# A joint run for the h of two groups, V0 in quads by other queues, and a later place for the loads of batch 2

## The chip, the cores and the metric

The kernel runs on one core of one Trainium2 chip. Five engines work side by side and meet at semaphores: TensorE (PE, matmuls; its weight loads are listed as PEld), VectorE (DVE), ScalarE (ACT), GpSimd (POOL) and SyncE (SP, which here only issues transfers). The metric is the device time of one execution in microseconds (us); less is better.

## The reference

```python
x = softmax-weighted causal convolution of x_in over 7 taps   # weights per head: 8 heads of 24 channels
xt = x.transpose(0, 2, 1)
h = xt @ U @ V                       # U: seq x 32, V: 32 x seq, along the sequence
u = x + h.transpose(0, 2, 1)
out = u + np.maximum(u @ w_ch1, 0.0) @ w_ch2     # 192 -> 768 -> 192
```

There are 8 batches of 4224 positions with 192 channels, all float32 at the kernel's edge.

## The kernel before

**Tiling.** A batch is 33 tiles of 128 positions. The 264 tiles of all batches form 33 groups of eight, so groups 0 to 3 lie wholly in batch 0. In the text below, y is the convolved x, tt is U^T y (32 x 192, kept four times on 128 partitions), h is V's part of tt, u = y + h, uT is u transposed (channels on partitions), and rl is the output of the first channel matmul after the relu.

**Stages.** The convolution is done by PE with banded weight matrices made at the start (line 369 for batches 0 and 1, line 339 with 32-row bands for the others, from a second, shifted copy `xb_sb` of x that POOL makes in lines 293 to 305). `tt_mm` (402), `tt_split`, `tt_sum` and `tt_done` make tt. `h_tiles` (457, 479) makes u for a group; `transp` (498) has SP issue a transposing transfer that makes uT. `w1` (554) multiplies uT by W1, and ACT and DVE evict it with the relu (568, 570); `w2` (583, 592, 600) multiplies by W2, adds u on DVE and has SP issue the output. All PSUM tiles come from one ring of eight banks (`bank`), in order of allocation.

**Groups 0 and 1** are made in another way, with no transposing transfer. `yT_part` (509) lets PE transpose y of a group into PSUM banks, through matmuls with an identity, half the tiles to partitions 0 to 63 and half to 64 to 127. `hT_part` (524) adds V0^T tt to the same banks with 32-row matmuls that all take tt and V0 from partitions 0 to 31, and evicts the sums to uT (256, 258). `parts` is a list of (channel block c, first tile, end tile, bank, evicting engine). Group 0 has five parts, group 1 three; the order on PE, with lines of the listing, is

```python
yT_part(0, parts0)      # 729
conv_piece(1); tt_mm; tt_split; conv_piece(2); ...
yT_part(0, more[0:1]); tt_late(ps0); yT_part(0, more[1:])
yT_part(1, parts1); tt_done(0, ps0)
hT_part(0, parts0 + more)
yT_part(1, rest); hT_part(1, parts1 + rest)
```

**What sets the order.** The schedule is written out by hand, each engine works through its instructions in program order. All loads of x, U, V and the weights are issued by POOL, in one queue, and convert float32 to bfloat16 on the way: x of batch 0 in three pieces with U between, then V0 (line 133), W1, the first part of batch 1, V, W2, the rest of batch 1. SP issues the small conv weight `w_sb` (61) first, and later the transposes and the outputs. A batch of x is four parts (`XP`), held in two buffers.

`SLOTS` says for each slot which groups go through `w1`, which through `w2`, and what stands between the pieces of `w2` (four pieces of two tiles for each group): h0 is u of group 0, d1 the convolution of batch 1, c2 that of batch 2, t and s make tt, x2:6 are six copies of POOL for batch 2, l2:3 is the load of part 3 of batch 2, held until the last `w2` piece issued so far is done. `LOADS` names loads that are held until a given (group, m) of `w1` is done. The loads of batch 2 stand in both: parts 0 and 1 behind the last m of `w1` of group 1, part 2 behind the first `w2` piece of group 0, part 3 behind its second.

Of the kernel before, what the change touches and what calls it, by code (L numbers as in the profile page):

```python
# [8 lines left out]
ACT = mybir.ActivationFunctionType  # L9
BF16 = mybir.dt.bfloat16  # L10
F32 = mybir.dt.float32
# [3 lines left out]
def kernel(  # L15
# [20 lines left out]
    GT = 8  # L36
# [3 lines left out]
    HB = P // 2  # L40
# [4 lines left out]
    cst = ctx.enter_context(tc.tile_pool(name="cst", bufs=1))  # L45
# [4 lines left out]
    uts = ctx.enter_context(tc.tile_pool(name="uts", bufs=5))  # L50
# [5 lines left out]
    def bank():  # L56
        return psp.tile([P, 512], F32, name="ps", tag="ps")


    w_sb = cst.tile([P, H, KC], F32, name="w_sb")  # L60
    nc.sync.dma_start(out=w_sb[:], in_=weight[:].partition_broadcast(P))
    xt = [None] * B
    yt = [None] * B

# [38 lines left out]
    def iota(t, pattern, base, mul):  # L103
# [20 lines left out]
        out=Ur[:, 0:nfull, :], in_=U4[0 : nfull * P, :].rearrange("(k p) c -> p k c", p=P)  # L124
# [4 lines left out]
        x_piece(k)  # L129


    V0_sb = cst.tile([R, 2 * GT * P], BF16, name="V0_sb")
    nc.gpsimd.dma_start(out=V0_sb[:], in_=moe_V[:, 0 : 2 * GT * P])
    W1_sb = cst.tile([P, 3, M4], BF16, name="W1_sb")
    for m0, m1 in ((0, 2 * P), (2 * P, M4)):
        for hf in range(2):
            nc.gpsimd.dma_start(
                out=W1_sb[HB * hf : HB * hf + HB, :, m0:m1],
                in_=moe_w_ch1[:, m0:m1].rearrange("(c k) m -> k c m", k=HB),
# [27 lines left out]
    for hh in range(2):  # L167
# [3 lines left out]
        out=dif[:], in0=dif[:], scalar1=rq[:, 0:1], scalar2=None, op0=ALU.add  # L171
# [5 lines left out]
        out=d_sb[:],  # L177
# [3 lines left out]
    )  # L181
    e_sb = cst.tile([P, H, KC], F32, name="e_sb")
    nc.scalar.activation(e_sb[:], d_sb[:], ACT.Exp)
    hot = cst.tile([P, KC, BW], BF16, name="hot")
    nc.vector.tensor_tensor(
        out=hot[:],
# [6 lines left out]
        out=ident[:], in0=fp[:], scalar1=float(P), scalar2=None, op0=ALU.is_equal  # L193
# [9 lines left out]
        out=c_sb[:].rearrange("p k h -> p h k"),  # L203
# [5 lines left out]
    for hh in range(2):  # L209
# [3 lines left out]
            out=pr[:],  # L213
# [8 lines left out]
        out=Eq[:], in0=efp[:], scalar1=rq[:, 1:2], scalar2=None, op0=ALU.is_equal  # L222
# [3 lines left out]
        out=fp[:], in0=fp[:], scalar1=R - 1, scalar2=None, op0=ALU.bitwise_and  # L226
# [3 lines left out]
        out=R4[:], in0=fp[:], scalar1=0.0, scalar2=None, op0=ALU.is_equal  # L230
# [23 lines left out]
    def evac(eng, out, in_):  # L254
        if eng == "A":
            nc.scalar.activation(out=out, in_=in_, func=ACT.Copy)  # L256
        else:
            nc.vector.tensor_copy(out=out, in_=in_)  # L258
# [135 lines left out]
    ttb = [[] for _ in range(B)]  # L394
# [25 lines left out]
    def tt_done(b, p):  # L420
        t = sml.tile([P, D], BF16, name="tt_sb", bufs=3)
        nc.vector.tensor_copy(out=t[:], in_=p[:, 0:D])
        ttb[b] = t
# [14 lines left out]
    uTt = [None] * NG  # L438
# [64 lines left out]
    def yT_part(g, parts):  # L503


        for c, i0, i1, p, _ in parts:
            for i in range(i0, i1):
                for hf in range(2):
                    nc.tensor.matmul(  # L509
                        out=p[HB * hf : HB * hf + HB, (i - i0) * P : (i - i0 + 1) * P],  # L510
                        lhsT=yt[0][:, GT * g + 4 * hf + i, HB * c : HB * c + HB],
                        rhs=ident[:],
                        start=(i == i0),
                        stop=False,
                        tile_position=(0, HB * hf),
                    )

    def hT_part(g, parts):

        uTt[g] = uts.tile([P, 4, 3, P], BF16, name="uT")  # L520
        for c, i0, i1, p, _ in parts:
            for hf in range(2):
                t0 = (2 * g + hf) * 4 * P
                nc.tensor.matmul(  # L524
                    out=p[HB * hf : HB * hf + HB, 0 : (i1 - i0) * P],
                    lhsT=ttb[0][0:R, HB * c : HB * c + HB],
                    rhs=V0_sb[:, t0 + i0 * P : t0 + i1 * P],
                    start=False,
                    stop=True,
                    tile_position=(0, HB * hf),  # L530
                )
        for c, i0, i1, p, eng in parts:
            evac(
                eng,
                uTt[g][:, i0:i1, c, :],
                p[:, 0 : (i1 - i0) * P].rearrange("p (i t) -> p i t", t=P),
            )

    RELU = ["AD", "AD", "AA", "AD", "AD", "AD"]
    RELU0 = ["AA", "AD", "AA", "AD", "AA", "AD"]  # L540
# [1 line left out]
    def w1(g, pat):  # L542
        rl = rls.tile([P, MC, 2, 4 * P], BF16, name="rl_sb")
        rlt[g] = rl
        ends = []
        lead = 2 if g == 0 else 1
        order = [(m, c) for c in range(3) for m in range(lead)]
        order += [(m, c) for m in range(lead, MC) for c in range(3)]
        pps = {}
        for m, c in order:  # L550
            if c == 0:
                pps[m] = [bank(), bank()]
            for hf in range(2):
                last = nc.tensor.matmul(  # L554
                    out=pps[m][hf][:],
                    lhsT=W1_sb[HB * hf : HB * hf + HB, c, m * P : (m + 1) * P],
                    rhs=uTt[g][HB * hf : HB * hf + HB, :, c, :],
                    start=(c == 0),
                    stop=(c == 2),
                    tile_position=(HB * hf, 0),  # L560
                )
            if c < 2:
                continue
            pp = pps[m]
            ends.append(last)
            for hf in range(2):
                if pat[m][hf] == "A":
                    nc.scalar.activation(out=rl[:, m, hf, :], in_=pp[hf][:], func=ACT.Relu)  # L568
                else:
                    nc.vector.tensor_scalar_max(out=rl[:, m, hf, :], in0=pp[hf][:], scalar1=0.0)  # L570
        return ends
# [38 lines left out]
    def x_load(b, q, after):  # L610
# [7 lines left out]

    SLOTS = [
        ([0], [], {}),  # L620
        ([1], [0], {0: ["h0"], 1: ["h3", "l2:2"], 2: ["l2:3"]}),
        ([2], [1], {0: ["d1", "h1"], 1: ["t1"], 3: ["s1"], 4: ["h4", "x2:6"]}),
        ([3], [2], {1: ["h5"], 3: ["h6"]}),
        (
            [4, 5],
# [41 lines left out]
        SLOTS.append((gs, gs, {p: [w for w in what if w] for p, what in at.items()}))  # L667
    assert nh == NG

    LOADS = {2: [(1, 5), (1, 5)], 3: [(4, 1), (4, 4), (5, 1), (5, 4)]}  # L670
    for b in range(4, B):
        g = 3 * b - 6
        LOADS[b] = [(g, 0), (g, 3), (g + 1, 0), (g + 1, 3)]

# [4 lines left out]
    def tt_late(p):  # L679

        for n, j in enumerate(late):
            nc.tensor.matmul(
                out=p[:, 0:D],
                lhsT=U4_sb[:, n, :, :].rearrange("p a r -> p (a r)"),
                rhs=yt[0][:, j, :],
                start=False,
                stop=(n + 1 == len(late)),
            )
# [10 lines left out]
    for r, (k0, k1) in KP[2].items():  # L699
        j = NB0 // 2 * r + k0  # L700
        nc.gpsimd.tensor_copy(
            out=U4_sb[:, o : o + k1 - k0, :, :],
            in_=U_sb[:]
# [9 lines left out]
    for q in range(4):  # L713
        src = moe_V[:, 0 : full * 8 * P].rearrange("r (k q t) -> r k q t", q=4, t=2 * P)
        nc.gpsimd.dma_start(
            out=V_sb[32 * q : 32 * q + 32, 0 : 2 * full, :].rearrange(
                "r (k a) t -> r k (a t)", a=2
            ),
            in_=src[:, :, q, :],
# [3 lines left out]
        out=V_sb[0:32, 2 * (NT // 8), :], in_=moe_V[:, (NT - 1) * P : NT * P]  # L723
# [1 line left out]
    W2_sb = cst.tile([P, MC, D], BF16, name="W2_sb")  # L725
    nc.gpsimd.dma_start(out=W2_sb[:], in_=moe_w_ch2[:].rearrange("(m p) d -> p m d", p=P))

    parts0 = [(0, 0, 2, bank(), "A"), (0, 2, 4, bank(), "D"), (1, 0, 4, bank(), "D")]
    yT_part(0, parts0)
    def conv_piece(k):  # L730
        for n, h in enumerate(range(0, H, 3)):
            for r in KP[k]:
                conv(0, h, min(3, H - h), [r], "AD"[n % 2], KP[k], {r: work[n]})
# [5 lines left out]
    ps0 = work[3]  # L739
    for n, part in enumerate(ttb[0]):  # L740
        nc.tensor.matmul(out=ps0[:, 0:D], lhsT=R4[:], rhs=part[:], start=(n == 0), stop=False)
    more = [(2, 0, 2, bank(), "A"), (2, 2, 4, bank(), "A")]
    yT_part(0, more[0:1])
    tt_late(ps0)
    yT_part(0, more[1:])
    parts1 = [(0, 0, 4, bank(), "A")]
    yT_part(1, parts1)
    tt_done(0, ps0)
    hT_part(0, parts0 + more)
    rest = [(c, 0, 4, bank(), "ADA"[c]) for c in (1, 2)]  # L750
    yT_part(1, rest)
    hT_part(1, parts1 + rest)
    band2 = cst.tile([P, H, QB], BF16, name="band2")
    for xp in XP[1:]:
        x_part(1, *xp)
    for r in range(4):
        q = slice(QB * r, QB * r + QB)
        for hh in range(2):
            nc.gpsimd.tensor_copy(
                out=band2[q, HQ * hh : HQ * hh + HQ, :],  # L760
                in_=bands[hh][q, :, HB * (r % 2) : HB * (r % 2) + QB],
# [86 lines left out]
```

## Time and profile before

| | |
|---|---|
| median of 3 runs | 325.0 us (324.93 to 325.19) |
| profiled execution, first to last instruction | 323.2 us |
| PE busy (share of the span) | 317.6 us (98%) |
| DVE / ACT / POOL busy | 268.6 / 170.0 / 142.7 us |
| granted clock of PE, mean | 1.000 |
| x of batch 0, first piece | issued from 1.27 us on, first conv matmul that needed it 9.63 us |
| L509 (y transposed), 48 matmuls | 0.22 us each |
| L524 (h of groups 0 and 1), 16 matmuls | 0.33 us each, 18.34 to 20.5 us |
| uT evictions of groups 0 and 1 | ACT 5, DVE 3 |
| loads of batch 2 issued | 29.29, 30.1, 30.95 and 32.66 us |

The profile is one execution, and its span leaves out what lies before the first and after the last instruction. Busy shares are over the whole span. A matmul's length contains the time it takes to leave the array, so matmuls that follow each other overlap in the profile, and the distance of their starts tells the pace. A transfer is told by its issue (on SP, ACT or POOL) and by the time to its landing.

### The profile page before, as it was taken

Reading aid. Unit: us, or ns where it says so; the run is one execution under the profiler, and the core shown is the slowest. Engines: PE = TensorE matmul, PEld = TensorE weight load, DVE = VectorE, ACT = ScalarE, POOL = GpSimd, SP = SyncE. Lnnn points to the kernel's source line nnn. Section 1 sums busy time; section 2 is a strip of 40 time slices with the busy share of each in tenths; the row PEclk is TensorE's granted clock in tenths of the full one; section 3 lists DMA queues with packets and bytes.
Section 4 is the critical chain, followed back from the end, with each engine's and each line's share of the span. In section 5 each row is a group of like instructions: output and inputs, shape, how many; then the busy total and the mean of one; then the engine's idle time right before and its main releaser. Section 6 shows DMA issues by size and latency. Waiting matters only on the chain.

```text
span 323.2 us, 9583 instructions
## 1 busy us (share of the span) xinstructions
PE 317.6 (98%) x3996; PEld 223.7 (69%) x3996; DVE 268.6 (83%) x551; ACT 170.0 (53%) x344; POOL 142.7 (44%) x111
## 2 busy tenths in 40 slices
PE   8999999999999999999999999999999999999995
PEld 3747676478677647866864884687797497487495
DVE  6769989987977986997898699789888897896863
ACT  1766724860874397088239609824903902912910
POOL 8764179728957983992897497000000000000000
PEclk9999999999999999999999999999999999999999
DMA  9999993999998999599499957138268059048035
GB/s 106 192 191 183 206 209 100 196 192 257 208 135 200 246 142 190 166 189 209 130 237 192 181 149 194 52 105 231 61 178 262 3 150 275 18 121 271 2 121 173
DMA packets 122906, 53.51 MB, mean 166 GB/s; under 512 B 87760, under 2 KB 122832, under 8 KB 122864
## 3 DMA queue, kind: packets, MB, share of 16 engines
q1 hardware_dynamic: 84528, 38.08, 45.4%
q0 software_dynamic: 38192, 14.73, 39.2%
q8 instruction: 31, 0.51, 0.7%
q10 hardware_dynamic: 144, 0.10, 0.1%
q14 instruction: 11, 0.09, 0.1%
HBM read 29.49 MB, written 25.95 MB: 172 GB/s over the span
## 4 chain that ended last, share of the span: by engine, by line
PE 92%; ACT 3%; DMA 2%; DVE 1%; issue 0%; POOL 0%; POOLq 0%
PE ps L583 42%; PE ps L554 39%; PE ps L339 3%; PE ps L457 3%; DMA x_sb<-in_x_dram 2%; PE ps L402 2%; ACT rl_sb L568 2%; PE ps L369 1%; ACT y_sb L256 1%; PE ps L509 1%; DVE u_sb L479 1%; DVE rl_sb L570 1%; PE ps L524 0%; PE ps L428 0%; POOL x_sb L79 0%
## 5 line engine op out<-in xcount | busy, mean ns | idle before, releaser
L568 ACT ACTIVATE rl_sb<-ps 128x512 bf16<-128x512 f32 x233 | 124.3, 604 | 108.0 <-PE ps L554 96.0
L583 PE MATMUL ps<-W_sb,rl_sb 128*128 128x192 bf16 x1584 | 141.2, 246 | 0.2
L583 PEld LDWEIGHTS <-rl_sb 128*128 128x128 bf16 x1584 | 128.3, 98 | 11.8 <-issue 11.5
L554 PE MATMUL ps<-uT,W_sb 64*128 64x512 bf16 x1188 | 131.7, 376 | 0.0
L570 DVE TENSOR_SCALAR rl_sb<-ps 128x512 bf16<-128x512 f32 x163 | 105.3, 688 | 15.7 <-PE ps L554 15.4
L554 PEld LDWEIGHTS <-W_sb 64*128 64x128 bf16 x1188 | 66.9, 94 | 60.4 <-issue 3.9
L592 DVE TENSOR_TENSOR out_sb<-ps,u_sb 128x384 f32<-128x384 f32 (+1 forms) x133 | 70.4, 551 | 25.5 <-PE ps L583 25.0
L305 POOL COPY xb_sb<-x_sb 32x3072 bf16<-32x3072 bf16 (+1 forms) x24 | 67.4, 2824 | 0.5
L479 DVE TENSOR_TENSOR u_sb<-y_sb,ps 128x192 bf16<-128x192 bf16 (+1 forms) x168 | 66.3, 461 | 0.0
L293 POOL COPY xb_sb<-x_sb 128x3072 bf16<-128x3072 bf16 x12 | 32.7, 2742 | 42.1 <-PE ps L339 32.2
L256 ACT ACTIVATE y_sb<-ps 128x384 bf16<-128x384 f32 (+4 forms) x90 | 38.3, 520 | 9.7 <-PE ps L339 7.4
L79 POOL DMA_DIRECT2D x_sb<-in_x_dram x32 | 27.0, 848 | 9.6 <-PE ps L457 3.8
L258 DVE CAST y_sb<-ps 128x408 bf16<-128x408 f32 (+4 forms) x36 | 19.1, 578 | 1.3 <-PE ps L369 1.0
L457 PE MATMUL ps<-tt_sb,V_sb 32*128 32x192 bf16 x264 | 12.4, 246 | 0.1
L339 PE MATMUL ps<-x_sb,band 64*32 64x384 bf16 x192 | 12.1, 333 | 0.0
L339 PE MATMUL ps<-xb_sb,band 64*32 64x384 bf16 x192 | 12.1, 332 | 0.0
L457 PEld LDWEIGHTS <-V_sb 32*128 32x128 bf16 x264 | 4.7, 92 | 7.3 <-issue 7.3
L416 ACT ACTIVATE tt_hi<-ps 128x192 bf16<-128x192 f32 x8 | 2.6, 330 | 11.9 <-PE ps L402 11.9
L369 PE MATMUL ps<-x_sb,band 64*64 64x240 bf16 (+3 forms) x192 | 8.0, 276 | 0.2 <-DMA x_sb<-in_x_dram 0.2
L339 PEld LDWEIGHTS <-band 64*32 64x32 bf16 x384 | 4.5, 89 | 5.2 <-issue 2.4
L153 PE MATMUL ps<-zz 128*128 128x512 f32 (+1 forms) x10 | 6.7, 816 | 1.1 <-DVE zz L143 1.1
L369 PEld LDWEIGHTS <-band 64*64 64x64 bf16 x192 | 6.0, 106 | 2.1 <-issue 1.4
(65 smaller groups left out, 71.3 us busy)
## 6 DMA issues: line engine op xcount, KB each, us to landing
out_dram<-out_sb SPq DMA_DIRECT2D x131, 192.0 KB, 2.7
x_sb<-in_x_dram POOLq DMA_DIRECT2D x14, 384.0 KB, 6.9
x_sb<-in_x_dram POOLq DMA_DIRECT2D x7, 432.0 KB, 6.7
x_sb<-in_x_dram POOLq DMA_DIRECT2D x7, 408.0 KB, 8.0
x_sb<-in_x_dram POOLq DMA_DIRECT2D x1, 504.0 KB, 7.3
uT<-u_sb SPq DMA_TRANSPOSE x31, 3.5
x_sb<-in_x_dram POOLq DMA_DIRECT2D x1, 480.0 KB, 5.6
W_sb<-in_moe_w_ch_dram POOLq DMA_DIRECT2D x2, 192.0 KB, 7.8
```

The lines of the kernel that those rows point to most:

```text
L79: return nc.gpsimd.dma_start(out=xt[b][HB * r : HB * r + HB, s0:s1, :], in_=x[b, blk * HB : (blk + s1 - s0) * HB, :].rearrange("(j p) d -> ...
L256: nc.scalar.activation(out=out, in_=in_, func=ACT.Copy)
L293: nc.gpsimd.tensor_copy(out=xbt[b][:, s0:s1, :], in_=xt[b][:, s0 + 1 : s1 + 1, :])
L305: nc.gpsimd.tensor_copy(out=xbt[b][q, s0:s1, :], in_=xt[b][q, s0:s1, :])
L339: nc.tensor.matmul(out=pp[r][QB * cg : QB * cg + QB, 0 : nk[r] * GS], lhsT=w[hr], rhs=t[hr, st : st + 2 * nk[r] - 1 : 2, hs], start=True, ...
L457: nc.tensor.matmul(out=banks[pr][:, a * D : (a + 1) * D], lhsT=V_sb[32 * q : 32 * q + 32, (j // 8) * 2 + j % 2, :], rhs=ttb[b][32 * q : 32 ...
L479: nc.vector.tensor_tensor(out=u_group(g)[:, i : i + n, :, hf, :], in0=yt[b][:, run[0] : run[0] + n, :].rearrange("p n (c k) -> p n c k", c=3),
L554: last = nc.tensor.matmul(out=pps[m][hf][:], lhsT=W1_sb[HB * hf : HB * hf + HB, c, m * P : (m + 1) * P], rhs=uTt[g][HB * hf : HB * hf + HB ...
L568: nc.scalar.activation(out=rl[:, m, hf, :], in_=pp[hf][:], func=ACT.Relu)
L570: nc.vector.tensor_scalar_max(out=rl[:, m, hf, :], in0=pp[hf][:], scalar1=0.0)
L583: last = nc.tensor.matmul(out=cps[:, a * D : (a + 1) * D], lhsT=rlt[g][:, m, hf, (i + a) * P : (i + a + 1) * P], rhs=W2_sb[:, m, :], start ...
L592: nc.vector.tensor_tensor(out=o[:, 0:n, :].rearrange("p n (c k) -> p n c k", c=3), in0=cps[:, 0 : n * D].rearrange("p (n c k) -> p n c k", ...
```

## The change

1. V0 is no longer loaded by POOL. Four transfers of 32 rows by 512 columns, issued at the start by SP (two) and ACT (two), bring it as float32 onto four blocks of 32 partitions, ahead of the first issue of x in the program. ACT casts it to bfloat16 in one instruction behind the exponential of the conv weights.
2. Groups 0 and 1 have three parts each, of one whole bank. `yT_part` of group 1 stands wholly ahead of the h matmuls. `hT_part` takes both groups at once: for each channel block four matmuls of 512 columns, one on each block of 32 rows (q), the halves of group 0 on q = 0 and 1, those of group 1 on q = 2 and 3. The evictions follow, group 0 first, each group by ACT, DVE, ACT.
3. The loads of batch 2 leave `LOADS`. Part 0 stands behind the third `w2` piece of group 0, parts 1 and 2 behind the fourth, part 3 behind the first `w2` piece of group 1.

```diff
     nc.sync.dma_start(out=w_sb[:], in_=weight[:].partition_broadcast(P))
+    V0_f = cst.tile([4 * R, 4 * P], F32, name="V0_f")
+    for q in range(4):
+        (nc.scalar if q % 2 else nc.sync).dma_start(
+            out=V0_f[R * q : R * q + R, :], in_=moe_V[:, 4 * P * q : 4 * P * (q + 1)]
+        )
...
-    V0_sb = cst.tile([R, 2 * GT * P], BF16, name="V0_sb")
-    nc.gpsimd.dma_start(out=V0_sb[:], in_=moe_V[:, 0 : 2 * GT * P])
...
     nc.scalar.activation(e_sb[:], d_sb[:], ACT.Exp)
+    V0_sb = cst.tile([4 * R, 4 * P], BF16, name="V0_sb")
+    nc.scalar.activation(out=V0_sb[:], in_=V0_f[:], func=ACT.Copy)
...
-    def hT_part(g, parts):
...
+    def hT_part(of):
+        for c in range(3):
+            for g in range(2):
+                p = of[g][c][1]
+                for hf in range(2):
+                    q = 2 * g + hf
+                    nc.tensor.matmul(
+                        out=p[HB * hf : HB * hf + HB, :],
+                        lhsT=ttb[0][R * q : R * q + R, HB * c : HB * c + HB],
+                        rhs=V0_sb[R * q : R * q + R, :],
+                        start=False,
+                        stop=True,
+                        tile_position=(R * q, HB * hf),
+                    )
+        for g in range(2):
+            uTt[g] = uts.tile([P, 4, 3, P], BF16, name="uT")
+            for c, p, eng in of[g]:
+                evac(eng, uTt[g][:, :, c, :], p[:].rearrange("p (i t) -> p i t", t=P))
...
-        ([1], [0], {0: ["h0"], 1: ["h3", "l2:2"], 2: ["l2:3"]}),
-        ([2], [1], {0: ["d1", "h1"], 1: ["t1"], 3: ["s1"], 4: ["h4", "x2:6"]}),
+        ([1], [0], {0: ["h0"], 1: ["h3"], 3: ["l2:0"], 4: ["l2:1", "l2:2"]}),
+        ([2], [1], {0: ["d1", "h1"], 1: ["t1", "l2:3"], 3: ["s1"], 4: ["h4", "x2:6"]}),
...
-    LOADS = {2: [(1, 5), (1, 5)], 3: [(4, 1), (4, 4), (5, 1), (5, 4)]}
+    LOADS = {3: [(4, 1), (4, 4), (5, 1), (5, 4)]}
...
-    parts0 = [(0, 0, 2, bank(), "A"), (0, 2, 4, bank(), "D"), (1, 0, 4, bank(), "D")]
-    yT_part(0, parts0)
+    parts0 = [(c, bank(), "ADA"[c]) for c in range(3)]
+    yT_part(0, parts0[0:2])
...
-    more = [(2, 0, 2, bank(), "A"), (2, 2, 4, bank(), "A")]
-    yT_part(0, more[0:1])
+    yT_part(0, parts0[2:])
     tt_late(ps0)
-    yT_part(0, more[1:])
-    parts1 = [(0, 0, 4, bank(), "A")]
+    parts1 = [(c, bank(), "ADA"[c]) for c in range(3)]
     yT_part(1, parts1)
     tt_done(0, ps0)
-    hT_part(0, parts0 + more)
-    rest = [(c, 0, 4, bank(), "ADA"[c]) for c in (1, 2)]
-    yT_part(1, rest)
-    hT_part(1, parts1 + rest)
+    hT_part([parts0, parts1])
```

More of the change, by code (lines that the diff above doesn't have):

```diff
@@ L503, in yT_part @@
     def yT_part(g, parts):
-        for c, i0, i1, p, _ in parts:
-            for i in range(i0, i1):
+        for c, p, _ in parts:
+            for i in range(4):
                 for hf in range(2):
                     nc.tensor.matmul(
-                        out=p[HB * hf : HB * hf + HB, (i - i0) * P : (i - i0 + 1) * P],
+                        out=p[HB * hf : HB * hf + HB, i * P : (i + 1) * P],
                         lhsT=yt[0][:, GT * g + 4 * hf + i, HB * c : HB * c + HB],
                         rhs=ident[:],
-                        start=(i == i0),
+                        start=(i == 0),
                         stop=False,
@@ L516, in yT_part @@
                     )
-    def hT_part(g, parts):
[L520 to L530, printed above, removed]
-                )
[L532 to L537, printed above, removed]
+    def hT_part(of):
[15 more added lines that the diff above has]
+            for c, p, eng in of[g]:
+                evac(
+                    eng,
+                    uTt[g][:, :, c, :],
+                    p[:].rearrange("p (i t) -> p i t", t=P),
+                )
     RELU = ["AD", "AD", "AA", "AD", "AD", "AD"]
```

## The prediction

> **What bounds the kernel now.** Read first: the page's busy times. TensorE (PE) is busy 317.6 of 323.2 us and its clock row is full throughout, so time can only come off where PE starts late or waits. Second: the chain of waits in order of time. From 81 us on it is PE alone, in a fixed period of 28 us per batch; whatever is won or lost before then reaches the end undiminished unless a transfer stands in between. The start of the chain:
>
> ```profile
> 2.29 7.30 DMA x_sb<-in_x_dram
> ...
> 17.47 0.18 issue
> 17.65 0.24 PE ps L682
> 17.89 0.46 PE ps L509 x12
> 18.35 0.83 PE ps L524 x10
> 19.18 0.57 PE ps L509 x16
> 19.75 0.76 PE ps L524 x6
> 20.51 1.23 PE ps L554 x10
> 21.74 3.04 ACT rl_sb L568 x6
> 24.79 0.04 issue
> 24.83 4.16 PE ps L554 x36
> ```
>
> The reader sees start and length of each piece: x must land (9.6 us), then PE runs to the h stage (L509 transposes y, L524 adds h: 18.35 to 20.51), then `w1` of group 0 fills its first banks, and for 3.04 us ScalarE (ACT), not PE, sets the pace, until its sixth rl eviction frees the bank with which `w1` of group 1 starts (24.83). Third, the timeline there and at the start (start, length, engine, line; idle time before in brackets):
>
> ```profile
> 10.60 0.45 PEld L369 LDWEIGHTS <-band 64*64 64x64 bf16 x20 [0.21 <-DVE band L258]
> 17.82 0.53 PE L509 MATMUL ps<-ident,y_sb 128*64 128x128 bf16 x12
> 19.68 0.83 PE L524 MATMUL ps<-V_sb,tt_sb 32*64 32x512 bf16 x6
> 20.12 1.08 ACT L256 ACTIVATE uT<-ps 128x512 bf16<-128x512 f32 x2 [0.35 <-PE ps L524]
> 21.73 3.54 ACT L568 ACTIVATE rl_sb<-ps 128x512 bf16<-128x512 f32 x7 [0.52 <-PE ps L554]
> 24.44 0.34 PE L457 MATMUL ps<-tt_sb,V_sb 32*128 32x192 bf16 x8
> ```
>
> ACT was idle 0.52 us before its rl run: it waited for PE. If uT is ready earlier, ACT's run begins earlier, and all after it moves by that. Fourth, the windows of the start (DMA share and GB/s last), and the timeline of the transfers of the middle:
>
> ```profile
> 2.50:3.00 0.50, 0.50 (x2) 0.06 (x1) 0.00 (x0) 0.00 (x0) 0.50 (x1) 1.00 0.09 20
> 3.00:3.50 0.50, 0.50 (x2) 0.27 (x1) 0.00 (x0) 0.00 (x0) 0.41 (x3) 1.00 0.86 52
> 4.50:5.00 0.50, 0.50 (x2) 0.33 (x1) 0.50 (x3) 0.25 (x1) 0.50 (x1) 1.00 1.59 191
> ```
>
> ```profile
> 41.04 1.45 SPq L498 DMA_TRANSPOSE uT<-u_sb  x1
> 45.35 2.74 POOL L293 COPY xb_sb<-x_sb 128x3072 bf16<-128x3072 bf16 x1 [1.41 <-DMA x_sb<-in_x_dram]
> 48.69 11.24 POOL L305 COPY xb_sb<-x_sb 32x3072 bf16<-32x3072 bf16 x4
> ```
>
> The DMA engines are nearly empty until 3.0 us (share 0.09, full is 1.6). The transpose for group 3, issued at 41.04, lands 5.6 us later, at 46.64, and `w1` of group 3 begins at 47.12: 0.48 us of slack. POOL's copies of batch 2 end at 59.93 and are first read at 66.88.
>
> **V0 by the hardware queues.** Two more issues on SP after w_sb's, two on ACT ahead of the table load, about 0.40 us each (w_sb's L61; ACT's own last issue took 0.38). ACT's table load ends at 2.8 instead of 2.03; its first work, e_sb, starts at 4.71 after 2.68 us idle, which hides it. SP has nothing else until 27.14. POOL loses one issue of 0.56 us, and V0's bytes leave the queue ahead of W1; W1's last part lands at 18.9 already, before `w1` (20.45), so this gains nothing. The new cast of 128x512 on ACT costs 0.60 (its uT evictions); it waits for V0, then stands before the band evictions at 8.03, with ACT idle from 4.96: hidden if V0 lands by 7.4, otherwise it delays the bands. The four transfers are 256 KB together. What they take from x is not in the trace. Upper bound: all in front of x at 191 GB/s, 1.37 us; lower: 0, in engines that are idle. w_sb, issued at 0.76 in the same queue, moved its bytes from 1.5 us on, and V0's four issues end by 2.0, so nearly all falls into the empty stretch and into x's ramp (52 of 191 GB/s at 3.0 to 3.5). I take 0.1, and the 0.21 us that PE waits for the second half of the bands at 10.60 covers it: 0 on the path.
> A rule against the placing: the Trainium skill, DMA: Bandwidth & Descriptors, section Issuing engines are not separate DMA queues, says that all queues share the same 16 engines, so that another queue saves only issue time. By it V0 costs x its bytes (up to 1.16 us after the cover); by the windows above the engines have nothing to do then.
>
> **The yT matmuls.** Eight instead of four L509 before `tt_late`: 12 of them started within 0.31 us at 17.82, 0.028 each, so `tt_late` and the cast of tt end 0.11 later. After `tt_late` 24 instead of 12: 17.93 + 0.17 + 24 x 0.028 + 0.21 of drain: the h run starts at about 18.83 instead of 18.34, +0.49. The 0.18 idle at 17.47 (0.34 late by the cadence before it) shows no releaser; it may stay or go: 0 to -0.34, I take 0.
>
> **The joint h run.** Sixteen L524 in two runs (0.83 + 0.76, with 16 L509 between, 0.57) become twelve of 512 columns. Pairs of 512 columns followed each other by 0.22 us (19.68, 19.92, 20.14). Four row tiles at once were seen at L457: eight matmuls of 192 columns, 0.25 us each alone, in 0.34. If four run together here too, three sets: 0.66 us; if not, six pairs 1.32. I take 0.66. The c0 banks are then ready at 18.83 + 0.45 = 19.28, c1 at 19.47, c2 at 19.68. Evictions: ACT now has four of 512 (two of 512 took 1.08: 0.60, then 0.48 each): 19.28 to 21.32, free for the next from 21.20. DVE has two, 19.47 to 20.81. `w1` starts when c0 is out, 19.93 instead of 20.45; waits for c1's bank to be emptied (20.21) and then runs at 0.109 per matmul (36 in 4.06), so that m = 0 is complete at 21.28. ACT's rl run begins at 21.28 instead of 21.73: **-0.45 us**, still back to back behind it, so `w1` of group 1 starts at 24.38. DVE is 0.45 earlier as well. The banks repeat at the same distance (eight allocations), so no new bank wait arises.
>
> **Batch 2 later.** Three of its loads move from 29.29, 30.1, 30.95 behind the third and fourth W2 piece, to about 33, 34, 35; the last from 32.66 to 42.5, each 0.85 of POOL issue plus the memset (0.17), which POOL's 3.83 idle covers. POOL is in order: behind the last load stand the copies of batch 2 and then batch 3's loads. Last landing 45.26 becomes about 49 (42.5 + 2.4 to first bytes, as 60.11 to 62.5, + 2.2 us for 408 KB at 191 GB/s, + 1 to 2 beside the outputs), copies end at about 63.6 instead of 59.93; read at 66.4: 2.8 us of slack. Batch 3's loads (last issue 64.23) go to about 66.3, and its copies end at 92.5 to 94.5 instead of 91.40, read at 94.6: just enough. 0 on the path.
>
> **Sum.** 0 + 0 - 0.45 + 0: span 323.2 - 0.45 = 322.75; the medians stand 1.8 us above the span (325.0), so 324.55, rounded to **324.5 us**. With the idle 0.34 gone too, 324.2; with V0 fully ahead of x, 325.7.
>
> **Rivals.** *The run isn't joint.* Row tiles 0 and 1 write the two halves of one bank at the same time, which no line of this profile does: L457 and L554 give each row tile a bank of its own. If matmuls of one bank follow each other, seven steps of 0.22 = 1.54 us replace three: c2 is ready at 20.6, ACT's four evictions end at 22.1, rl starts at 22.0: +0.25, 325.2. For: nothing like it in the trace; against: pairs of column halves shared a bank at L524 without loss.
> The Trainium skill, TensorEngine Tiling (Array Packing), Restrictions and Gotchas, speaks against the change: different row tiles cannot access the same PSUM bank simultaneously. By it the sum is this rival's.
> *The transpose of group 3 comes late* (the slower one). PE arrives 0.45 earlier, which leaves 0.03 of the 0.48 slack. The stream of batch 2, which in three cases (drained at 29.3, 43.7, 72.6) ended 3.0 us before a transpose landed (32.24, 46.64, 75.6), drains at about 44.2 with three loads; if the fourth follows without a gap, at 47.1, and the transpose lands at 50.1 where 46.67 is needed. Price 0.5 to 3.4 us, middle 1.95: 324.55 + 1.95 = 326.5. It decides from a landing after 46.67 + 0.45. Against: the fourth's first bytes are due at 44.9, after the drain.
> *Batch 3's copies come late* at 94.6 for want of loads: 1 to 2 us, 326.0; its margin is 0.1 to 2.1.
>
> **Numbers.** Within 0.2% is 0.65 us, about what a measurement of this kernel can tell from no change. Forecast 0.58, own range 323.9 to 325.0; as the idle 0.34 and DVE's earlier start may add, 0.34 of it lies below 324.35 and 0.24 within. Not joint 0.14 (0.13 within, 0.01 slower). Transpose 0.20 (0.19 slower, 0.01 within). Copies 0.08, slower. So faster 0.34, within 0.38, slower 0.28. The range goes from 323.9 to 326.6, the rivals' middles included.
>
> **What would show it.** Right: twelve L524 within 1.05 us, starting near 18.8; ACT's first rl near 21.3; no idle PE before 47. Wrong: L524 spread over 1.5 us (not joint); PE waiting on uT before `w1` of group 3 with a transpose landing past 47; PE L339 waiting on xb_sb near 66 or 94; the first L369 after 9.8 (V0 delays x). The forecast fails if any of these waits exceeds 0.45 us.

## The result and the profile after

The changed kernel took 339.8 us (median of 6 runs, 332.85 to 343.17) beside 325.0 us for the kernel before (324.93 to 325.42). Four of its runs lie more than 1.5% above its fastest, and the ratios here and below leave such runs out, so that a ratio can be lower than the quotient of the medians. The ratio is 1.0297, with an interval of 1.0249 to 1.0346, that is 8.1 to 11.2 us more. It is slower, and the forecast of 324.5 us was wrong. The profiled execution has a span of 335.0 us, 11.8 more than before. The table follows the delay through it: the time at which PE starts each group's `w1`, and the end of its last matmul. Three of the experiments stand beside it.

| PE, us | before | after | batch 2's loads put back | only batch 2's loads moved | only the joint run |
|---|---|---|---|---|---|
| start of `w1` of group 0 | 20.45 | 21.65 | 22.60 | 20.56 | 19.92 |
| start of `w1` of group 2 | 33.76 | 35.01 | 35.96 | 33.88 | 33.77 |
| start of `w1` of group 3 | 47.12 | 49.30 | 49.32 | 48.45 | 47.40 |
| start of `w1` of group 6 | 81.09 | 86.50 | 83.28 | 86.96 | 83.23 |
| start of `w1` of group 9 | 109.39 | 120.78 | 111.58 | 119.85 | 112.09 |
| end of the last matmul | 319.79 | 331.16 | 321.97 | 330.24 | 322.55 |

After group 9 nothing more is lost. Before it there are four losses: 1.2 us at the start, 0.9 at group 3, 3.2 between groups 3 and 6, 6.0 between groups 6 and 9. Differences below 0.3 us between two executions tell little: in the kernel before and in experiments 2, 7, 11 and 12, which are equal up to there, `w1` of group 0 starts anywhere from 20.30 to 20.56.

**The start.** The timeline of PE in the changed kernel (start, length, engine, line, operation, count; idle time before in brackets):

```profile
9.64 0.29 PE L374 MATMUL ps<-x_sb,band 64*64 64x240 bf16 x2
11.49 1.83 PE L374 MATMUL ps<-x_sb,band 64*64 64x240 bf16 x62 [1.55 <-DMA x_sb<-in_x_dram]
...
19.27 0.57 PE L691 MATMUL ps<-y_sb,U_sb 128*128 128x192 bf16 x5 [0.30 <-issue]
19.77 0.86 PE L514 MATMUL ps<-ident,y_sb 128*64 128x128 bf16 x24
20.56 0.84 PE L531 MATMUL ps<-V_sb,tt_sb 32*64 32x512 bf16 x12
21.65 2.63 PE L563 MATMUL ps<-uT,W_sb 64*128 64x512 bf16 x22 [0.25 <-ACT uT L261]
```

L374, L514, L531 and L563 are the old L369, L509, L524 and L554. PE stands still for 1.55 us, for x: its first piece is complete at 11.45 instead of 9.59. The twelve h matmuls, on the other hand, run together in 0.84 us from the first start to the last end. The windows of the changed kernel at the two stretches that the prediction looked at (bounds in us, five engines' busy times, granted clock, DMA share, GB/s):

```profile
2.50:3.00 0.50, 0.50 (x2) 0.07 (x1) 0.00 (x0) 0.46 (x1) 0.50 (x1) 1.00 0.50 158
3.00:3.50 0.50, 0.50 (x2) 0.27 (x1) 0.00 (x0) 0.00 (x0) 0.41 (x3) 1.00 0.58 112
4.50:5.00 0.50, 0.50 (x2) 0.34 (x1) 0.21 (x1) 0.00 (x0) 0.50 (x1) 1.00 1.56 175
5.50:6.00 0.50, 0.50 (x2) 0.33 (x1) 0.47 (x4) 0.50 (x2) 0.50 (x2) 1.00 1.33 154
```

V0 does begin in the empty stretch (158 GB/s where there were 20), but it isn't over there: its four transfers land between 4.56 and 5.32 us. From 4.5 us on both together move 175 GB/s where x alone moved 191, and x by itself is still lower at 5.5 (154 instead of 194).

**The middle.** The chain of waits of the changed kernel (start, length, what), from 42 us on:

```profile
42.29 6.96 DMA uT<-u_sb
...
49.30 2.76 PE ps L563 x23
```

```profile
72.58 9.72 DMA out_dram<-out_sb
...
84.49 2.08 PE ps L592 x12
86.57 4.62 PE ps L563 x27
...
91.25 0.50 POOL xb_sb L300
...
101.89 3.09 POOL xb_sb L310
...
105.02 1.22 PE ps L344 x19
```

Three things that stood in no chain before now stand in it: a transpose, an output transfer, and POOL's copies. The timelines of POOL and of SP in the changed kernel tell why:

```profile
34.39 0.82 POOL L84 DMA_DIRECT2D x_sb<-in_x_dram  x1 [8.44 <-PE ps L592]
35.38 1.65 POOL L84 DMA_DIRECT2D x_sb<-in_x_dram  x2 [0.17 <-issue]
44.79 0.87 POOL L84 DMA_DIRECT2D x_sb<-in_x_dram  x1 [7.75 <-PE ps L592]
...
53.42 2.74 POOL L298 COPY xb_sb<-x_sb 128x3072 bf16<-128x3072 bf16 x1 [2.73 <-DMA x_sb<-in_x_dram]
56.23 0.50 POOL L300 COPY xb_sb<-x_sb 32x384 bf16<-32x384 bf16 x1
56.77 11.25 POOL L310 COPY xb_sb<-x_sb 32x3072 bf16<-32x3072 bf16 x4
68.07 0.17 POOL L79 MEMSET x_sb<- 64x96 uint32 x1
68.19 3.35 POOL L84 DMA_DIRECT2D x_sb<-in_x_dram  x4
83.42 2.74 POOL L298 COPY xb_sb<-x_sb 128x3072 bf16<-128x3072 bf16 x1 [11.87 <-DMA x_sb<-in_x_dram]
```

```profile
69.14 3.35 SPq L503 DMA_TRANSPOSE uT<-u_sb  x1
72.58 10.80 SPq L609 DMA_DIRECT2D out_dram<-out_sb  x9
```

In the kernel before, the loads of batch 3 and this transpose read:

```profile
60.11 1.63 POOL L79 DMA_DIRECT2D x_sb<-in_x_dram  x2
...
67.32 2.92 SPq L498 DMA_TRANSPOSE uT<-u_sb  x1
```

POOL is one queue. Part 3 of batch 2 is issued at 44.79 and lands at 53.30 (32.66 and 45.30 before), the copies wait for it and end at 68.0 (59.9 before), and only then come batch 3's loads: 68.19 (60.11 before). They land until 88.32 (74.77 before), their copies end at 104.97, and PE's conv of batch 3 is there at 101.26: it waits 3.76 us. The transpose of 69.14 is under that stream from the start and lands at 81.13, 12.0 us after its issue (8.3 before); the outputs issued behind it on SP's queue land later still, so DVE has no free output buffer, PE none of DVE's evictions, and `w1` of group 6 starts 5.4 us late.

The waits are not the whole loss. After each of the last two PE was granted half its clock, for 3.4 us each time. PE's timeline at the two waits, and the windows behind them (clock third from the end):

```profile
83.04 0.76 PE L462 MATMUL ps<-tt_sb,V_sb 32*128 32x192 bf16 x3 [1.44 <-DVE out_sb L601]
...
105.02 0.49 PE L344 MATMUL ps<-xb_sb,band 64*32 64x408 bf16 x1 [3.76 <-POOL xb_sb L310]
```

```profile
84.00:86.00 2.00, 1.83 (x15) 1.64 (x15) 1.53 (x4) 0.00 (x0) 2.00 (x1) 0.57 1.31 244
86.00:88.00 2.00, 2.00 (x14) 0.75 (x14) 2.00 (x5) 0.01 (x1) 0.16 (x1) 0.57 1.20 304
104.00:106.00 2.00, 0.98 (x23) 0.34 (x22) 0.06 (x1) 0.40 (x2) 2.00 (x3) 0.70 1.43 217
106.00:108.00 2.00, 2.00 (x19) 1.65 (x12) 0.99 (x2) 1.28 (x4) 0.61 (x1) 0.50 0.94 86
```

The clock is 0.50 from 84.30 to 87.71 and from 104.78 to 108.19. Half of what PE worked in these two stretches, some 3.3 us, is an estimate of their price. It closes the account of the last loss: between groups 6 and 9, 3.76 us of waiting and 0.6 + 1.6 us at half the clock make 5.96 of the 6.0.

### The profile page after: what moved, and what is told of

It reads as the page before. It is cut to its first block, busy times and chain, and to the rows that moved or that the text cites. A ratio compares the mean times of both kernels' runs of the same rounds, so it can differ in the third digit from the quotient of the medians.

```text
span 335.0 us, 9582 instructions
## 1 busy us (share of the span) xinstructions
PE 320.3 (96%) x3992; PEld 223.3 (67%) x3992; DVE 268.9 (80%) x550; ACT 170.0 (51%) x344; POOL 142.3 (42%) x110
## 4 chain that ended last, share of the span: by engine, by line
PE 82%; DMA 8%; POOL 4%; ACT 3%; DVE 2%; issue 1%; DVEq 0%; POOLq 0%
PE ps L592 37%; PE ps L563 36%; POOL xb_sb L310 3%; PE ps L344 3%; DMA out_dram<-out_sb 3%; DMA x_sb<-in_x_dram 3%; PE ps L462 3%; DMA uT<-u_sb 2%; PE ps L407 2%; ACT y_sb L261 1%; DVE u_sb L484 1%; PE ps L374 1%; POOL x_sb L84 1%; ACT rl_sb L577 1%; DVE rl_sb L579 1%
## 5 line engine op out<-in xcount | busy, mean ns | idle before, releaser
L592 PE MATMUL ps<-W_sb,rl_sb 128*128 128x192 bf16 x1584 | 143.0, 248 | 0.3
L592 PEld LDWEIGHTS <-rl_sb 128*128 128x128 bf16 x1584 | 129.8, 98 | 12.6 <-issue 11.8
L563 PE MATMUL ps<-uT,W_sb 64*128 64x512 bf16 x1188 | 131.9, 377 | 1.1 <-DMA uT<-u_sb 0.9
L563 PEld LDWEIGHTS <-W_sb 64*128 64x128 bf16 x1188 | 65.0, 94 | 64.0 <-issue 4.3
L344 PE MATMUL ps<-xb_sb,band 64*32 64x384 bf16 (+1 forms) x192 | 12.9, 343 | 3.8 <-POOL xb_sb L310 3.8
L462 PE MATMUL ps<-tt_sb,V_sb 32*128 32x192 bf16 x264 | 13.1, 246 | 1.8 <-DVE out_sb L601 1.4
L374 PE MATMUL ps<-x_sb,band 64*64 64x240 bf16 (+3 forms) x192 | 7.9, 275 | 1.6 <-DMA x_sb<-in_x_dram 1.6
L421 ACT ACTIVATE tt_hi<-ps 128x192 bf16<-128x192 f32 x8 | 2.7, 332 | 11.9 <-PE ps L407 11.9
L374 PEld LDWEIGHTS <-band 64*64 64x64 bf16 x192 | 6.1, 106 | 3.2 <-issue 2.7
```

What stands on the lines that cost most here:

```text
L344: nc.tensor.matmul(out=pp[r][QB * cg : QB * cg + QB, 0 : nk[r] * GS], lhsT=w[hr], rhs=t[hr, st : st + 2 * nk[r] - 1 : 2, hs], start=True, ...
L462: nc.tensor.matmul(out=banks[pr][:, a * D : (a + 1) * D], lhsT=V_sb[32 * q : 32 * q + 32, (j // 8) * 2 + j % 2, :], rhs=ttb[b][32 * q : 32 ...
L563: last = nc.tensor.matmul(out=pps[m][hf][:], lhsT=W1_sb[HB * hf : HB * hf + HB, c, m * P : (m + 1) * P], rhs=uTt[g][HB * hf : HB * hf + HB ...
L592: last = nc.tensor.matmul(out=cps[:, a * D : (a + 1) * D], lhsT=rlt[g][:, m, hf, (i + a) * P : (i + a + 1) * P], rhs=W2_sb[:, m, :], start ...
```

## The experiments

The kernel before was run beside each group of runs; its medians there were 324.93, 325.08, 325.11 and 325.02 us, and ratios are against these. Most of the last six kernels scattered more than the first eight.

**1. Batch 2's loads put back** into the changed kernel (`LOADS` and the two slots as before).

> The changed kernel with batch 2 loaded where it was before. Theory (the late loads of batch 2 cost the large part; V0 ahead of x costs 1.86 us of x's landing, of which 0.2 is covered and the joint run gives back 0.5 to 0.65): 326.2 us, between 325.7 and 326.8, first L374 conv matmul on x at 11.4, no wait of PE on xb_sb or on out_sb. Rival (the late start alone pushes the later loads and copies past their readers, whatever the place of batch 2's loads): 331 or more.

Measured 327.1 us, ratio 1.0065 (1.0049 to 1.0081). All waits of the middle are gone; what is left is the start: x at 11.59, `w1` of group 0 2.2 us late, and the same 2.2 at the last matmul. Of the 0.9 us above the expectation most is clock: in this execution the first conv took 2.73 us instead of 1.98, as PE's granted clock fell after the wait for x. Its windows (columns as above):

```profile
11.50:12.00 0.50, 0.37 (x16) 0.37 (x19) 0.00 (x0) 0.00 (x0) 0.13 (x1) 1.00 1.64 188
12.00:12.50 0.50, 0.50 (x28) 0.50 (x21) 0.00 (x0) 0.32 (x1) 0.50 (x2) 0.89 1.62 193
12.50:13.00 0.50, 0.50 (x20) 0.50 (x15) 0.21 (x1) 0.50 (x2) 0.18 (x1) 0.50 1.60 191
```

**2. Only batch 2's loads moved**, in the kernel before.

> The kernel before with only batch 2's loads moved as in the change. Theory: POOL's copies of batch 2 end near 64 to 68, batch 3's loads start only then, its copies end near 100, outputs wait for their transfers: 332 to 340 us. Rival (it takes the late start as well): 325 to 326.5. Prediction's own sum for this part: no change, 325.0.

Measured 335.2 us, ratio 1.0314 (1.0298 to 1.0329). One part of the change gives the whole of the middle. Its chain of waits:

```profile
41.15 7.25 DMA uT<-u_sb
...
71.94 10.82 DMA out_dram<-out_sb
...
100.89 3.09 POOL xb_sb L305
...
104.02 0.78 PE ps L339 x16
```

These are the transpose, the outputs and POOL's copies of the changed kernel, at nearly the same times, with an undisturbed start.

**3. The joint run with V0 as bfloat16 by four POOL issues**, at V0's old place, loads of batch 2 as before.

```diff
+    for q in range(4):
+        nc.gpsimd.dma_start(
+            out=V0_sb[R * q : R * q + R, :], in_=moe_V[:, 4 * P * q : 4 * P * (q + 1)]
+        )
```

> The kernel before with the joint h run alone: V0 in four quads by POOL as bfloat16 at V0's old place, all loads of x as before. Theory (the joint run is joint): x lands at 9.6 as before, twelve h matmuls within 1.05 us, first rl eviction at 21.1 to 21.3, 324.4 us (324.2 to 324.7). Rival (matmuls of one bank follow each other): twelve h matmuls over 1.7 us, 325.2. If three more POOL issues delay W1 past 20: also 325 or more, with PE waiting on W_sb.

Measured 328.3 us, ratio 1.0099 (1.0082 to 1.0116): a miss. The start came as forecast (h run at 18.84, `w1` of group 0 at 19.96, ACT's first rl at 21.24). But three more issues made POOL's queue late with everything behind them: the last load of batch 1 landed at 34.52 instead of 30.91, and the transpose of group 2, issued at 27.14, at 37.17 instead of 32.27. `w1` of group 2 waited 3.13 us for it, and then ran at half the clock for 3.4 us.

**4. Batch 3's loads ahead of batch 2's copies**, in the changed kernel, to take them out of POOL's chain.

> The changed kernel with batch 3's four loads issued ahead of POOL's copies of batch 2 (behind the last W2 piece of group 1) instead of behind them. Theory (the large loss is batch 3's loads standing behind late copies): the waits of DVE on out_dram and of PE on xb_sb near 80 to 105 go; what stays is 1.2 us from the start and 0.9 us from the transpose of group 3: 327 to 328. Rival (batch 2's late landing itself makes the loss): 332 or more.

Measured 333.6 us, ratio 1.0268 (1.0245 to 1.0290): a miss, too. The waits near 80 and 105 went, and the wait moved to the transposes: those issued at 51.02 and 57.65, which took 5.3 and 3.2 us in the changed kernel, took 11.0 and 11.4 now that loads ran beside them. So the loads cost wherever a transpose falls under them, and POOL's chain is only one of the two ways.

**5. The joint run with V0 by one POOL issue**, at its old place.

```diff
+    nc.gpsimd.dma_start(
+        out=V0_sb[:], in_=moe_V[:, 0 : 16 * P].rearrange("r (q t) -> q r t", q=4)
+    )
```

> The kernel before with the joint h run alone; V0 in four quads of 512 columns, as bf16, by ONE GpSimd issue at V0's old place in the queue (the earlier try had four issues there and cost 3.3 us). If those four issues were to blame (GpSimd was late with W1, V and batch 1, and its stream never ran empty for the transpose of group 2): that transpose lands near 32.3 again, w1 of group 0 starts 19.96 (20.45 before), and the time is 324.4 (-0.5). If 128 rows of 2 KB in the source are slow whatever issues them: x's second and third piece and W1 come 0.5 to 1 us later, 325 to 326. If the joint run itself upset what follows: 328 as with four issues.

Measured 326.0 us, ratio 1.0041 (1.0023 to 1.0058). The four issues were most of experiment 3's loss. V0 in 128 rows landed at 17.10 where it had landed at 15.11, batch 1 came 0.4 to 0.8 late, and the transpose of group 2 landed at 34.55.

**6. V0 on SP's queue, held until the first conv group has ended**, with its cast behind the third conv piece, loads of batch 2 as before.

> The changed kernel with batch 2's loads as before, and V0 still float32 by the hardware queue, but all four quads on SP's queue, held until the first convolution group has ended (about 10.5 us), cast on ACT behind the third convolution piece. If it was V0 ahead of x that cost 2.2 us in the run with the loads put back (327.1; x's first piece at 11.59, w1 of group 0 at 22.60): x lands 9.6, w1 of group 0 starts 19.96 and the time is 324.4. Rival: beside x's later pieces V0 takes as much from them as ahead of the first (1.9 us), and the wait moves to the second or third piece of the convolution or to the cast: 326 to 327.

Measured 327.7 us, ratio 1.0077 (1.0064 to 1.0090). x was on time (9.67), `w1` of group 0 started 0.27 earlier than before, and group 2 at 33.95, 0.19 later; the transpose landed at 33.91. The rival is nearer, though the wait it named isn't the one that came. The end is 1.7 us late in the profiled execution, and 1.5 of it arise between group 2 and group 9.

**7. Batch 2's part 3 behind W2 of group 0 as well**, in the kernel before, so that only the other three parts' delay is left.

> The kernel before with batch 2's loads moved behind W2 of group 0 as in the change, but its part 3 there too (in the change it waits for group 2's w1). If GpSimd's chain is what costs (copies of batch 2 begin when part 3 has landed, 53 in the change, 45 before; batch 3's loads stand behind them): part 3 lands near 49, the copies end near 64 (68 in the change, 60 before), batch 3's convolution waits 1 us or less, and the time is 326 to 328. If it is the transposes behind a full load queue: the one of group 3 (issued 41.2) lands with the stream's end plus 3 us, 51 to 53 instead of 48.4, w1 of group 3 waits 4 us, and the time is 329 to 331. The change's loads alone gave 335.2.

Measured 330.6 us, ratio 1.0169 (1.0153 to 1.0184): the second theory. POOL's copies ended at 64.9, and batch 3's conv waited for nothing. The transpose of group 3 landed at 50.66, and `w1` of group 3 started 3.6 us late. There it lost 2.5 more, since after 3.6 us without work PE was granted half its clock; the windows of this kernel:

```profile
48.00:50.00 2.00, 0.00 (x0) 0.00 (x0) 1.33 (x5) 0.00 (x0) 1.16 (x1) 0.95 1.33 124
50.00:52.00 2.00, 1.30 (x8) 0.47 (x10) 0.00 (x0) 0.00 (x0) 1.70 (x1) 0.50 1.06 343
52.00:54.00 2.00, 2.00 (x12) 0.70 (x10) 1.18 (x2) 1.12 (x2) 1.90 (x3) 0.50 1.32 138
54.00:56.00 2.00, 2.00 (x12) 0.74 (x10) 0.21 (x1) 1.16 (x3) 2.00 (x1) 0.50 0.42 95
```

So the deferral costs by the transposes where part 3 comes with the others, and by POOL's chain as well where it comes last.

**8. V0's four hardware-queue loads added ahead of x and not read**, in the kernel before.

> The kernel before with the four float32 loads of V0 by SP and ACT ahead of x added and nothing read from them (V0 is also still loaded as before; h runs as before). If the 256 KB ahead of x are what moves the start: x's first piece lands at 11.4 to 11.6 (9.59), w1 of group 0 starts at 22.3 to 22.9 (20.45), and the time is 326.8 to 327.4. If x was late for another reason (w_sb, or V0's row layout in the h run): 324.9.

Measured 328.3 us, ratio 1.0101 (1.0081 to 1.0121); the profiled span is 3.1 above that of before. x landed at 11.59, `w1` of group 0 started at 22.56, 2.11 late, and the last matmul ran 2.5 late. The transfer alone explains the start.

**9 and 10. Experiments 6 and 5 with batch 2's parts 0 and 1 held a little longer** (behind the sixth and the ninth matmul of W2 of group 0), to widen the pause in POOL's stream.

> The run with V0 held on SP's queue (327.7), with batch 2's parts 0 and 1 issued behind the sixth matmul of W2 of group 0 instead of behind the last W1 matmul of group 1, about 0.5 us later. Theory: the transpose of group 2 needs a pause in GpSimd's stream between batch 1's last landing (31.0) and batch 2's first packets; the kernel before has 30.91 and an issue at 29.29, the held run 31.0 and 29.07, and its transpose landed 33.91 instead of 32.27. With the issue at 29.5 the pause is back: the transpose lands 32.3 to 32.6, w1 of group 2 starts 33.5 to 33.6 (33.95 held, 33.76 before), and the time is 324.7 to 325.5. Rival: the 128 KB more that V0 moves as float32 make the stream late as a whole, whatever the pause: part 3 of batch 2 lands at 46 or later (45.30 before), batch 3's loads with it, outputs wait behind the transpose of group 8, and it stays at 327 to 328.

> The run with the joint h run alone and V0 by one GpSimd issue (325.96 against 325.08), with batch 2's parts 0 and 1 behind the ninth matmul of W2 of group 0, about 0.75 us later, as batch 1 lands there at 31.34. Theory of the pause: the transpose of group 2 lands 32.3 to 32.8 instead of 34.55, w1 of group 2 starts 33.6 instead of 34.60, part 3 of batch 2 lands 45.3 to 46, and the time is 324.7 to 325.3. Rival, the whole stream is late by the 0.9 us that V0 in 128 rows costs: w1 of group 3 or the outputs behind the transpose of group 8 wait, 325.8 to 326.5.

Measured 328.2 us, ratio 1.0073 (1.0039 to 1.0108), and 327.2 us, ratio 1.0056 (1.0027 to 1.0084). The transposes of group 2 landed at 33.89 and 34.42, no earlier than without the hold. A later issue alone doesn't help; my theory of the pause, as put there, falls.

**11. Batch 2's part 0 issued earlier**, in the kernel before, so that there is no pause.

```diff
-    LOADS = {2: [(1, 5), (1, 5)], 3: [(4, 1), (4, 4), (5, 1), (5, 4)]}
+    LOADS = {2: [(1, 2), (1, 5)], 3: [(4, 1), (4, 4), (5, 1), (5, 4)]}
```

> The kernel before with one number changed: part 0 of batch 2 is issued behind the third block of group 1's W1 instead of the sixth, some 2.5 us earlier, so that GpSimd's stream has no pause between batch 1 and batch 2. Theory of the pause: the transpose of group 2 (issued 27.14, landed 32.27) lands 34.5 or later, w1 of group 2 starts 34.6 to 37 instead of 33.76, and the kernel is slower by an EARLIER load: 325.8 to 328. Rival, what counts is when batch 2 lands (each us earlier is a us earlier for the copies and for batch 3): 324.0 to 324.9.

Measured 328.4 us, ratio 1.0057 (1.0017 to 1.0098). The ten runs spread from 325.8 to 331.4 us and the profiled one took 329.9, so its chain is that of one of the longer ones:

```profile
27.02 9.95 DMA uT<-u_sb
...
37.01 3.09 PE ps L554 x15
```

A load 2.1 us earlier makes the kernel slower: with the stream running on, the transpose took 9.95 instead of 5.13 us in this execution. That the stream delays it is shown; that a pause is what it needs, and how long a one, isn't, as experiments 9 and 10 issued batch 2 later for nothing.

**12. Batch 3's loads later**, in the kernel before: the first two issued 2.0 us later, the third 1.5, the last 0.4.

> The kernel before with batch 3's loads alone issued later, behind the second and third block of group 5's W1 (about 62 instead of 60.11). Nothing else moves. Theory of the second half of the loss: the stream's end moves from 74.8 to 77 to 78, the transpose of group 8 (issued 67.3, landed 75.64) lands with it plus 1 to 3 us, the outputs behind it on SP's queue hold the vector engine's buffers, w1 of group 6 starts 1 to 2.5 us after 81.09, batch 3's copies end 2 to 3 us later and its convolution waits at 95: 326 to 328. Rival: these 2 us are slack (batch 3 is read at 95): 324.9 to 325.3.

Measured 325.5 us, ratio 0.9994 (0.9972 to 1.0015): no difference, a miss. The transpose beside them landed at 77.08 instead of 75.64, and `w1` of group 6 started at 80.92, not later. So the kernel has at least the 1.4 us to spare by which this transpose landed later; experiment 5, where it landed at 78.76, lost 0.5 between groups 4 and 6, and the changed kernel, whose loads of batch 3 were issued 8.1 us late, is far outside.

**13. The joint run alone**, in the kernel before: V0 loaded as before, three of its quarters then copied on chip to the other row blocks, by DVE and ACT in idle time.

```diff
+    for q in range(1, 4):
+        evac("DDA"[q - 1], V0_sb[R * q : R * q + R, :], V0_l[:, 4 * P * q : 4 * P * (q + 1)])
```

> The kernel before with the joint h run and nothing of its transfers changed: V0 loaded as before (bf16, 32 rows, one GpSimd issue), then three of its quarters copied on chip onto row blocks 1 to 3 (two by the vector engine in its idle 16.8 to 17.9, one by ACT). If the joint run is worth its 0.45 to 0.49 at the end: x lands 9.6, the h run starts 18.84, w1 of group 0 19.96 (20.45 before), all later waits as before, 324.5. Rival: batch 2's loads, tied to the end of group 1's W1, are issued 0.45 earlier behind a batch 1 that lands no earlier, and the transpose of group 2 comes late again (34 instead of 32.27), so w1 of group 2 at 34 or later: 325.3 to 326.5.

Measured 326.7 us, ratio 1.0046 (1.0025 to 1.0066): the rival. The start of the h run (18.83), ACT's first eviction of uT (19.27) and its first rl (21.19) are those of the forecast. Then its chain of waits reads:

```profile
24.70 1.94 DVE u_sb L479 x4
26.66 7.07 DMA uT<-u_sb
33.77 4.06 PE ps L558 x36
37.83 3.17 PE ps L369 x62
41.05 6.30 DMA uT<-u_sb
...
71.44 9.03 DMA out_dram<-out_sb
```

The transpose of group 2 is issued 0.48 us earlier than before and lands 1.46 later, at 33.73. The 0.53 us won are gone at group 2. The transfers between 28 and 35 us, in 40 slices, are first those of the kernel before, then of this one (busy tenths, and what was moved):

```profile
DMA  9999999999522223999999999999999999999999
GB/s 191 193 193 195 193 282 200 256 238 88 31 29 36 42 48 48 282 291 287 295 283 165 171 180 189 189 197 195 191 195 191 242 163 173 167 154 149 169 173 197
```

```profile
DMA  9999999999964269990400000089999999999999
GB/s 191 195 191 195 231 180 195 228 249 211 102 73 55 35 107 364 268 227 18 4 0 1 9 9 9 10 193 290 229 191 195 191 195 191 195 191 197 189 197 182
```

Before, one stretch at a low rate (29.6 to 30.8), and then the transpose runs through. Here there is a second one, in which the transfers stand nearly still for 1.4 us (31.1 to 32.5, 0 to 18 GB/s) in the middle of the transpose.

That takes the gain; the loss comes later. The profiled execution took 327.5 us, 0.8 above the median, and its last matmul ends 2.8 us late. At group 5 `w1` is on time (60.34 in both); 2.1 us arise before group 6, where PE waits 0.92 us for DVE, which waits for the output transfer of the last row of the chain. The transpose of group 8, issued at 67.32 as before, landed at 79.25 instead of 75.64. Five executions show what the kernel bears there: 9.9 us from issue to landing (experiment 12) cost nothing between groups 5 and 6, 10.6 (experiment 5) 0.5 us, 11.0 (6) 0.9, 11.9 (13) 2.1 and 12.2 (14) 3.2. Why this transpose took 11.9 us here and 9.9 beside the later loads of experiment 12 stays open.

**14. The same with batch 2's parts 0 and 1 held** behind the sixth matmul of W2 of group 0.

> The same with batch 2's parts 0 and 1 behind the sixth matmul of W2 of group 0, about 0.5 us later, so that they are issued at 29.3 as before. If the joint run's gain was lost to the earlier issue in the run without this: the transpose of group 2 lands 32.3, w1 of group 2 starts 33.3, 324.5. If the gain is lost to something else (the pause of the transpose that the runs with the joint run all show near 31 to 32.5): w1 of group 2 at 33.9 or later, 325 to 326.

Measured 327.3 us, ratio 1.0073 (1.0049 to 1.0096). The parts were issued at 29.83 instead of 28.81, the transpose landed at 33.70 all the same. So it isn't the earlier loads that take the gain back.

No kernel here beat the one before.

## Why the prediction was wrong

**V0 by the hardware queues, 0 on the path: wrong, and the first step that failed.** It was to fall into the empty stretch and into x's ramp, and only a part did, as it landed between 4.56 and 5.32 us. x's first piece came 1.86 us late (2.00 in experiment 8), against an upper bound of 1.37 and 0.21 of cover. The bound let V0 move 256 KB at x's full 191 GB/s; together they reached 112 to 158 between 2.5 and 3.5 us, and x by itself was still at 154 at 5.5 us. The rule that I weighed against the windows was the better guide: the Trainium skill, DMA: Bandwidth & Descriptors, section Issuing engines are not separate DMA queues, has all queues share the same engines. Its direction holds here; the size, 2.1 us at `w1` of group 0, is above what I worked out from it (1.16).

**The yT matmuls (+0.49) and the idle 0.34 that stays: right.** Where V0 was loaded by POOL at its old place and landed about as early as before (experiments 3, 13 and 14) the h run starts at 18.84, 18.82 and 18.95, where 18.83 was put. The terms as written add up to 18.98, since 17.93 is already the start of the yT run and the 0.17 stands in it; without it they make 18.81. An idle 0.30 before the last U matmuls is in the changed kernel, 0.33 in experiment 13 and 0.49 in experiment 14.

**The joint run, 0.66 us in three sets: right; -0.45 at the end: wrong.** Experiment 13 has starts at 18.82, 19.06 and 19.28, c0 ready at 19.27 (19.28), `w1` at 19.92 (19.93), rl at 21.19 (21.28). The rival that the run isn't joint falls. What failed is "all after it moves by that": at group 2 the gain is gone, since the transpose that `w1` waits for is limited by transfers and not by PE. The end is even later than before, by 0.8 to 2.1 us (ratio 1.0025 to 1.0066), and in the trace that arises at the outputs behind the transpose of group 8, for which the sum had no term. I had looked at the slack of group 3's transpose only, 0.48 us, and not at group 2's, which landed at 32.27 for a start at 33.76.

**Batch 2's loads, 0 on the path: wrong, and the largest step**, some 10 us by experiment 2. The landing of part 3 was put at 49 and was 53.3 (52.4 with the start undisturbed): its issue came at 44.79 instead of 42.5, and at 43.68 in experiment 2 with the start undisturbed, and it took 8.5 us to land instead of 6.5. The copies of batch 2 ended at 68.0, not 63.6, and those of batch 3 at 104.97, not 92.5 to 94.5, when PE had been ready for them since 101.26. Two things were missing from the sum altogether: the wait for the transpose at 69 under batch 3's stream and the outputs behind it on SP's queue, and the half clock after PE's waits, some 3.3 us in the changed kernel.

**The rivals.** The late transpose of group 3 (0.5 to 3.4 us) came: it landed at 49.26, and cost 0.9, 1.3 in experiment 2, 3.6 in experiment 7. Batch 3's late copies (1 to 2 us) came in the changed kernel as a wait of 3.76, which with the stretches of half clock made 6.0. Each was priced as if it came alone and everything else held; they share one cause, a later stream of loads, and came together.

## What to carry to other kernels

A load that is issued later is not only needed later: ask which loads and copies stand behind it on its queue, and which other transfers then fall beside it. Find, for each transfer that PE waits for, what it shares the engines with, and price the moves by that, group by group; slack at one place says nothing of the next. A wait of PE may cost more than its length: here 3.76 us of waiting were followed by 3.4 us at half the clock. And a gain on PE ahead of a wait for a transfer counts only as far as that wait lets it through.

## What the hardware showed that I had not expected

A transposing transfer does not share evenly with POOL's loads. Alone it takes 3.2 us (49.45 to 52.64 before); under a full stream none or few of its packets move until the stream gives way, and it took 8.3 before (67.32), 12.0 in the changed kernel, 9.95 in experiment 11.

In all 16 traces a 16 KB transfer of the instruction queue runs beside the transpose of group 2, and the other transfers fall below 60 GB/s and come back 0.7 to 0.9 us after its end: it ran from 29.04 to 29.98 in the kernel before (low until 30.75), 30.67 to 31.84 in experiment 13 (32.6) and 30.88 to 32.30 in experiment 8 (33.05), which has no joint run. The transpose landed 1.4 to 2.4 us after that transfer's end in every trace but that of experiment 11, where the loads held it up. So the second standstill is not a mark of the joint run; it goes with the time of the instruction transfer. That the one stops the other was not tried on its own, nor what sets that time, and both stay open; it would explain why holding the loads changed nothing.

After a wait of PE the granted clock fell to 0.50, for 3.4 us each time and 6.8 in experiment 7. It did so after every wait of 2.0 us or more (2.01 to 3.76 us, in experiments 2, 3, 4, 7, 9 and 11 and the changed kernel), and after three shorter ones: 1.00 us in experiment 14, 1.44 in the changed kernel and 1.63 for x in experiment 1. It kept 1.00 after others of up to 1.92 us, the 1.55 for x in the changed kernel among them. What decides between them is not shown.

Four row tiles wrote at once here, two of them to each bank, and the twelve matmuls of 512 columns took 0.84 us. The Trainium skill, TensorEngine Tiling (Array Packing), Restrictions and Gotchas, says that different row tiles cannot access the same PSUM bank at the same time; with the two row tiles on different halves of the bank's partitions these runs show no price for it.
